# Row maxima ahead of attention, P.V in longer runs, and SyncE in written order in a fused attention and gMLP block

## The chip, the cores and the metric

The kernel runs on one core of a Trainium2 chip. The metric is device time of one execution in microseconds. TensorE (PE, with its weight loads PEld), VectorE (DVE), ScalarE (ACT), GpSimd (POOL) and SyncE (SP) run side by side; SyncE issues nearly all DMAs, ScalarE a few.

## The reference

One block over a sequence of S = 2048 rows, D = 576, in float32. `x` is normalised by row (a layer norm without weights). Side A is attention with 32 heads of 18 columns, causal with a window of 256. Side B is a gated MLP: `z = gelu(xn @ w_in)` of 4608 columns, the second half normalised by row, mixed over the sequence by `w_sp` (2048 x 2048) plus a bias, multiplied with the first half, and projected back. The result is `x + s * silu(g)`.

```python
qkv = (xn @ wqkv).reshape(B, S, 3, H, Dh)              # transposed to 3, B, H, S, Dh
scores = einsum("bhqd,bhkd->bhqk", q, k) * Dh ** -0.5  # masked to 0 <= q - k < 256
s = einsum("bhqk,bhkd->bhqd", softmax(scores), v) @ wo
z = gelu(xn @ w_in)
z1, z2 = z[..., :Fh], layernorm(z[..., Fh:])
g = (z1 * (einsum("ts,bsf->btf", w_sp, z2) + b_sp[None, :, None])) @ w_out
return x + s * silu(g)
```

## The kernel before

All large products are done in float32r with operands split in a high and a low part (ScalarE copies the high part, VectorE subtracts to get the low one), three matmuls each. The program has these stages:

1. Up to about 207 us: row norm, transposes, the q and k projection to DRAM (`st_d`) and the values to `v_d`.
2. To about 448 us: **z2**, the second half of the MLP's first projection, six column pieces (`pc`) of sixteen row blocks (`s`). Beside it GpSimd forms the four sums of `w_sp` blocks (`sp_combos`, tiles a11 to a22) that a Strassen-like spatial product needs. In the last piece, two row-maximum steps of attention unit 0 stand in each row block.
3. To about 1001 us: **attention**, in 16 units (`UNITS`: 8 groups of four heads, for the first half of the queries and then the second). A unit has 8 (first half) or 10 key blocks of four heads (`j`): 32 or 40 score items. For each, TensorE makes the transposed scores (`tps`, two PSUM buffers), ScalarE the exponential into `pt`, GpSimd the mask (two affine selects per key block), and TensorE then P.V into `ops`, four heads side by side in 32 columns each. Between the items TensorE fills in the matmuls of **z1** (`fill`, 1008 matmuls of 512 columns, in chunks of 14), the MLP's first half, whose gelu comes later.
4. To about 1697 us: the **spatial product**, 168 steps `m` of 18 matmuls (4.1 us) in three groups. Each needs a weight block `spr`, split into `sph` and `spl`, and a z block, split into `zh` and `zl`. `load_w(m + 4)` and `split_step(m + 2)` are called in step m; `pump` loads normalised z blocks (`zr`) for later products.
5. The output projections.

The **row maximum** (`row_max`) runs one unit ahead: 32 steps (4 heads, 8 query blocks), each a score matmul in `sp` (two PSUM buffers) and a masked maximum on VectorE into `mx` (`junk` takes the values); then one transpose of `mx`, its negative split in two rows (`mhl`), which go through DRAM (`m_d`) into two extra rows of the q tiles (`att<-m_d`), so that the score matmul subtracts the maximum by itself. With an empty step and the transpose a unit has `RMN = 34` steps.

The **divisor**: the values carry a column of ones, so that P.V also gives the row sums. `finish(u)` copies them out of `ou` to a tile `den` by DMA, VectorE takes the reciprocal, and that goes through DRAM (`r_d`) into a broadcast tile `rp` (of the last unit into a slot of `att`). VectorE multiplies `ou` by it, and four DMAs store to `o_d`.

The **order** in attention is written by hand for PE, POOL, DVE and ACT (`manual_schedule`): what the Python code issues first stands first on its engine. `spend` adds nominal durations to a clock, and `after(ns, fn)` issues fn once that clock has passed. SyncE is not in that list, so a scheduler places the DMAs of attention; in the spatial product SyncE stands in written order too. Each unit loads the q and k tiles of later heads with `load_pair` (eight DMAs each) into five rotating slots `att`. In a unit, the row maxima are paced over its first 70% (`RM1`), P.V blocks wait in `todo` and are issued when two are there (`PVN`), and z1 matmuls fill up to a target. Before unit 0 stand `HEAD = 28` z1 matmuls.

## Time and profile before

| | |
|---|---|
| runs | 2001.71 us median of 3 (1999.58 to 2002.24) |
| the profiled execution | 1998.85 us, span 1997.1 us, mean granted clock 0.995 |
| TensorE busy | 1954.4 us (98%) in 11096 matmuls |
| VectorE, ScalarE, GpSimd busy | 1055.0, 899.3, 289.1 us |
| spatial product, matmuls | 3 x 1008 of 128x512, idle before them 5.5 and 3.7 us |
| row maximum on VectorE | 448 of 384 columns, 553 ns each; 64 of 256 columns, 420 ns |
| exponential on ScalarE | 384 of 384 columns, 493 ns each |
| P.V matmuls | 512 of 384 columns, 448 of 256, 448 of 128 |

A row of a timeline or of the chain of waits begins with its start and its duration; the brackets give the idle time of the engine before it and what ended that. A row of waits reads: who waited for whom, microseconds in total, times, longest. PE is a matmul, PEld the weight load of the next one, which normally runs under the matmul before it. TensorE's busy time includes that its matmuls overlap, so lost time is read from the distance of one matmul's start to the next.

### The profile page before, as it was taken

To read this page: it belongs to the slowest core of one execution; us is meant where nothing else is said; L and a number is where in the kernel's file an instruction comes from. 1 tells how busy PE (TensorE), PEld (TensorE's weight loads), DVE (VectorE), ACT (ScalarE), POOL (GpSimd) and SP (SyncE) were. 2 spreads that over 40 slices of the span, in tenths; PEclk is the share of its full clock that TensorE was granted. 3 is DMA by queue.
4 is the path that set the end of the run, shared out by engine and by line. 5 is a ranking of instruction groups with operands and counts; after the bars stand their busy time and mean duration, and the time that the engine had idled before them with its cause. 6 is when DMAs were issued, how large, how long until landed. Compare 5 with 4: busy or idle time off the path is not lost.

```text
span 1997.1 us, 30611 instructions
## 1 busy us (share of the span) xinstructions
PE 1954.4 (98%) x11096; PEld 1647.0 (82%) x11096; DVE 1055.0 (53%) x2260; ACT 899.3 (45%) x1655; POOL 289.1 (14%) x360
## 2 busy tenths in 40 slices
PE   6999999999999999999999999999999999999998
PEld 5889999996777777777678887888888887999998
DVE  5411233366565656565148758676865675623222
ACT  4222322215555565656665466646554445422221
POOL 5000365102323223323200000000000000000000
PEclk9999999999999999999999999999999999999999
DMA  8655799424454655553376577857775567844441
GB/s 249 181 146 164 249 350 349 155 78 129 132 153 140 149 152 149 133 153 105 121 267 225 167 263 252 262 178 244 240 256 171 188 200 259 285 142 146 135 149 56
DMA packets 218983, 375.57 MB, mean 188 GB/s; under 512 B 43216, under 2 KB 115792, under 8 KB 218704
## 3 DMA queue, kind: packets, MB, share of 16 engines
q1 hardware_dynamic: 200880, 344.41, 55.4%
q10 hardware_dynamic: 17952, 29.21, 4.0%
q8 instruction: 87, 1.43, 0.3%
q14 instruction: 64, 0.52, 0.1%
HBM read 260.45 MB, written 112.83 MB: 187 GB/s over the span
## 4 chain that ended last, share of the span: by engine, by line
PE 85%; DMA 6%; DVE 5%; ACT 2%; issue 1%; SPq 0%; DVEq 0%; ACTq 0%
PE acc L926 27%; PE po L1018 12%; PE mm L444 11%; PE mm L650 10%; PE mm L306 5%; PE sp L394 5%; PE tps L513 5%; PE ops L536 4%; PE vps L463 3%; PE wops L988 2%; DVE spl L209 1%; DVE cb L874 1%; DVE z1t L855 1%; DMA a<-in_w_sp_dram 1%; DMA zr<-z_d 1%
## 5 line engine op out<-in xcount | busy, mean ns | idle before, releaser
L926 PE MATMUL acc<-sph,zh 128*128 128x512 f32 x1008 | 395.0, 392 | 5.5 <-ACT sph L209 5.5
L926 PE MATMUL acc<-spl,zh 128*128 128x512 f32 x1008 | 394.5, 391 | 3.7 <-DVE spl L209 3.4
L926 PE MATMUL acc<-sph,zl 128*128 128x512 f32 x1008 | 394.2, 391 | 0.0
L398 DVE CUSTOM_DVE_ANT_0 junk<-sp,band 128x384 bf16<-128x384 f32 (+1 forms) x512 | 265.5, 536 | 172.2 <-PE sp L394 164.9
L517 ACT ACTIVATE pt<-tps 128x384 f32<-128x384 f32 (+2 forms) x576 | 248.6, 439 | 179.0 <-PE tps L513 168.7
L444 PE MATMUL mm<-b,z1wh 128*128 128x512 f32 x648 | 248.4, 400 | 0.0
L926 PEld LDWEIGHTS acc<-spl,zh 128*128 128x128 f32 x1008 | 190.0, 188 | 47.5 <-DVE spl L209 7.3
L926 PEld LDWEIGHTS acc<-sph,zh 128*128 128x128 f32 x1008 | 189.9, 188 | 47.0 <-ACT sph L209 7.1
L209 DVE TENSOR_TENSOR spl<-spr,sph 128x1024 fp32r<-128x1024 f32 x166 | 202.7, 1221 | 40.0 <-ACT sph L209 39.7
L926 PEld LDWEIGHTS acc<-sph,zl 128*128 128x128 f32 x1008 | 189.8, 188 | 40.5
L513 PE MATMUL tps<-att 128*128 128x384 f32 (+1 forms) x576 | 192.5, 334 | 5.6 <-DMA att<-m_d 3.9
L650 PE MATMUL mm<-z2wh,b 128*128 128x384 f32 x720 | 192.1, 335 | 1.8 <-ACT zt L660 1.8
L394 PE MATMUL sp<-att 128*128 128x384 f32 (+1 forms) x512 | 181.8, 360 | 2.3 <-DVE mx L398 0.9
L209 ACT ACTIVATE sph<-spr 128x1024 fp32r<-128x1024 f32 x166 | 173.7, 1046 | 15.8 <-DMA spr<-in_w_sp_dram 14.9
L209 ACT ACTIVATE zh<-b 128x384 fp32r<-128x384 f32 x144 | 75.0, 521 | 197.4 <-PE acc L926 193.4
L1018 PE MATMUL po<-b,yh 128*128 128x288 f32 x896 | 155.7, 296 | 0.0
L209 DVE TENSOR_TENSOR zl<-b,zh 128x384 fp32r<-128x384 f32 x144 | 79.6, 553 | 124.8 <-ACT zh L209 124.8
L444 PE MATMUL mm<-b,z1wl 128*128 128x512 f32 x360 | 143.3, 398 | 0.0
L513 PEld LDWEIGHTS tps<-att 128*128 128x128 f32 x576 | 108.8, 189 | 41.3 <-issue 16.6
L444 PEld LDWEIGHTS mm<-b,z1wh 128*128 128x128 f32 x648 | 120.6, 189 | 25.8 <-issue 12.9
L661 DVE BATCH_NORM_STATS2 st<-zt 128x6 f32<-128x384 f32 x96 | 53.5, 559 | 166.8 <-ACT zt L660 166.8
L650 PE MATMUL mm<-z2wl,b 128*128 128x384 f32 x400 | 133.7, 334 | 0.0
(148 smaller groups left out, 2877.0 us busy)
## 6 DMA issues: line engine op xcount, KB each, us to landing
spr<-sc_d SPq DMA_DIRECT2D x96, 512.0 KB
spr<-in_w_sp_dram SPq DMA_DIRECT2D x72, 512.0 KB
zr<-z_d SPq DMA_DIRECT2D x136, 192.0 KB
st_d<-qkhl SPq DMA_DIRECT2D x72, 256.0 KB
z_d<-zt ACTq DMA_DIRECT2D x48, 384.0 KB
z1t<-z_d SPq DMA_DIRECT2D x72, 256.0 KB
y_d<-z1t SPq DMA_DIRECT2D x72, 256.0 KB
yr<-y_d SPq DMA_DIRECT2D x48, 384.0 KB
```

Source lines behind the costliest of these rows:

```text
L209: job()
L306: pe.matmul(ps, w, r, start=n == 0, stop=n == len(pl) - 1)
L394: pe.matmul(ps[:, :w], q_of(u, j)[:, i * P:(i + 1) * P], k_of(u, j)[:, k0:k0 + w], start=True, stop=True)
L398: dve.tensor_tensor_reduce(out=junk[:, :w], in0=ps[:, :w], in1=band[:, m0:m0 + w], scale=1.0, scalar=-3.0e38, op0=ALU.add, op1=ALU.max, ac ...
L444: pe.matmul(ps, w, r, start=n == 0, stop=n == len(pl) - 1)
L463: pe.matmul(ps[:, i, :288], r, w[:, i * 288:(i + 1) * 288], start=n == 0, stop=n == len(pl) - 1)
L513: pe.matmul(ps[:, :m * P], k_of(u, j)[:, (kb - base) * P:(kb - base + 1) * P], q_of(u, j)[:, (a - lo) * P:(a - lo + m) * P], start=True, s ...
L517: act.activation(pt[:, j, d0:d0 + n * P], ps[:, (qa - a) * P:(qa - a + n) * P], AF.Exp, scale=scale)
L536: pe.matmul(o_ps[c][32 * j:32 * j + 32, (lo - 4 * c) * P:(hi - 4 * c + 1) * P], vgs[u][:, kb - k0, j * VW:j * VW + 32], pt[:, j, (lo - kb) ...
L650: pe.matmul(ps[:, :ZW], r, wt, start=n == 0, stop=n == len(pl) - 1)
L926: pe.matmul(acc[j], z[:, ps], w[:, cs], start=s == i == 0 and n in OPENS, stop=s == 7 and i == 2, skip_group_check=True)
L1018: pe.matmul(po[i][:, a, :288], y[:, i * P:(i + 1) * P], w[:, a * 288:(a + 1) * 288], start=f == 0 and m == 0, stop=f == NF - 1 and m == 2)
```

## The change

**Row maximum.** All units' steps form one `stream`. It starts in the last 21 row blocks of z2 (two steps each, 42 in all: unit 0's 34 and eight, `LEAD`, of unit 1), and keeps eight steps ahead through all of attention, spread evenly over each unit. Both the fifth and the fourth slot are opened and cleared inside z2, on GpSimd, where the tiles of `sp_combos` were; so these are paced two row blocks in three instead of one in two. The maxima are stored 0.9 us of the clock behind the transpose and read back 1.8 us later. `HEAD` becomes 6.

**P.V.** `PVN` is four (two in the last unit), with five `pt` tiles. `burst` first issues the waiting `extras` and then all P.V blocks. The copy out of `ops` is issued 0.1 us of the clock later.

**extras.** The splits of the next z1 weights, the reciprocals and the divisions are put in a list, and issued at `j == 1` of each key block (one) or ahead of a run (five). The reciprocal is queued 3.6 us behind the divisor's `finish`, whose DMA stands at 0.9; before it was at 10 us. The division is queued 9.5 us behind the load of `rp`.

**SyncE** joins the written order in attention (`HEADS`), so each DMA is issued by `after` where its data should be there.

**Third spatial step.** The pool of steps 2, 5, 8... opens where the attention tiles were, `load_w(2)` and `split_step(2)` stand beside the last z1 matmuls. **pump** keeps up to four units, or five z blocks, in flight instead of two units.

```diff
-RM0 = 0.0
-RM1 = 0.70
 RMN = 34
-PVJ = 3
-PVN = 2
+LEAD = 8
+PVN = 4
+NPT = 5
-GAP = 8
-TAIL = 50 + 2 * GAP
-HEAD = 28
+GAP = 7
+TAIL = 66
+HEAD = 6
+HEADS = ENGINES | {ET.Activation, ET.SP}
...
-    def pump(n, depth=2):
+    def pump(n):
         for _ in range(n):
-            if flying and (len(flying) >= depth or not units):
-                form, got = flying.pop(0)
+            need = units[0][2] if units else 9
+            if flying and (len(flying) == 4 or sum(f[2] for f in flying) + need > 5):
+                form, got, _ = flying.pop(0)
                 form(got)
...
                 def put_max():
                     sp.dma_start(m_d[u], f32(m))
+                    after(1800, get_max)
+                def get_max():
                     rows = m_d[u].rearrange("(n j i) q -> n j (i q)", n=2, j=4)
...
-                after(500, put_max)
+                after(900, put_max)
...
+            def extra(n):
+                for _ in range(n):
+                    while extras and not extras[0]:
+                        extras.pop(0)
+                    if extras:
+                        extras[0].pop(0)()
...
                 def invert():
                     dve.reciprocal(den, den)
-                    sp.dma_start(r_d[u].rearrange("h (a b) -> (h a) b", b=HS // 32), den)
+                    after(600, lambda: sp.dma_start(r_d[u].rearrange("h (a b) -> (h a) b", b=HS // 32), den))
+                    after(2800, spread)
+                def spread():
                     sp.dma_start(rp, r_d[u].unsqueeze(1).to_broadcast([4, 32, HS]))
+                    after(9500, lambda: queue([divide]))
                 def divide():
                     dve.tensor_tensor(ou, ou, rp, ALU.mult)
+                    after(1500, store)
...
-                after(700, lambda: sp.dma_start(den, ou[DH::32, :]))
-                    after(10000, invert)
-                    after(24000, divide)
+                after(900, lambda: sp.dma_start(den, ou[DH::32, :]))
+                after(3600, lambda: queue([invert]))
...
+                stream = (step for u in range(NU) for step in row_max(u))
...
+                            if n in (4, 9) and pc * NS + s >= 6 * NS - (RMN + LEAD) // 2:
+                                next(stream)
...
+                def burst():
+                    extra(5)
+                    while todo:
+                        pv(*todo.pop(0))
+                    spend(250)
+                fill(HEAD)
...
+                        z = have + (want - have) * f - done
+                        r = min(RMN * (u + 1 + f) + LEAD, RMN * NU) - maxed
+                        while z >= 0.5 or r >= 0.5:
+                            if z >= 0.5:
                                 fill(1)
+                                z -= 1
+                            if r >= 0.5:
+                                next(stream, None)
+                                maxed += 1
+                                r -= 1
+                            if z < 1.5 and j == 3 and len(todo) >= (PVN if u < NU - 1 else 2):
+                                burst()
...
+                        if j == 1:
+                            extra(1)
...
+                work.close()
+                wpools[2] = open_pool(sets, "w2", side="right")
+                load_w(2)
+                fill(12)
+                split_step(2)
                 for _ in z1:
                     spend(MM)
...
-        for m in range(2, 4):
-            load_w(m)
+        load_w(3)
...
-            split_step(m + 2)
+            if m:
+                split_step(m + 2)
```

TensorE in the middle of a first-half unit, around a run of P.V (`ops`; `mm` is z1, `sp` the row maximum, `tps` the scores), before:

```order
L513 MATMUL tps<-att_4040 128x384
L444 MATMUL mm<-b_98,z1wh 128x512
L394 MATMUL sp<-att_1208 128x384 x2
L536 MATMUL ops<-pt,vg 32x256 x4
L536 MATMUL ops<-pt,vg 32x128 x8
L536 MATMUL ops<-pt,vg 32x256 x4
L513 MATMUL tps<-att_1210 128x384
```

and now:

```order
L526 MATMUL tps<-att_3464 128x384
L447 MATMUL mm<-b_95,z1wh 128x512
L394 MATMUL sp<-att_1205 128x384
L549 MATMUL ops<-pt_4499,vg 32x384 x4
L549 MATMUL ops<-pt_4556,vg 32x384 x4
L549 MATMUL ops<-pt,vg 32x256 x4
L549 MATMUL ops<-pt,vg 32x128 x8
L549 MATMUL ops<-pt,vg 32x256 x4
L447 MATMUL mm<-b_98,z1wh 128x512
```

A run holds the P.V of four key blocks instead of two, and the two `sp` in a row are gone: a z1 matmul stands between them.

VectorE near the end of a first-half unit, around the division (`ou<-ou,rp`; `junk` is the row maximum of one step, `mhl` the maxima of a unit, `z1wl` a weight split), before:

```order
L453 TENSOR_TENSOR z1wl<-z1raw,z1wh 128x256
L407 TENSOR_SCALAR mhl<-sp 32x128
L408 SCALAR_TENSOR_TENSOR mhl<-sp,mhl 32x128
L453 TENSOR_TENSOR z1wl<-z1raw,z1wh 128x256
L453 TENSOR_TENSOR z1wl<-z1raw,z1wh 128x128
L562 TENSOR_TENSOR ou<-ou,rp 128x1024
L398 ISA junk,mx<-sp,band 128x256
```

and now:

```order
L407 TENSOR_SCALAR mhl<-sp 32x128
L408 SCALAR_TENSOR_TENSOR mhl<-sp,mhl 32x128
L398 ISA junk,mx<-sp,band 128x256
L398 ISA mx 128x1
L398 ISA junk,mx<-sp,band 128x256
L398 ISA mx 128x1
L583 TENSOR_TENSOR ou<-ou,rp 128x1024
L398 ISA junk,mx<-sp,band 128x384
```

The division stood behind a unit's last row maximum with no other until the next unit; now it stands between two steps of the stream.

SyncE where attention ends (`spr` are weights of the spatial product, `den<-oul` the last unit's divisors, `o_d<-oul` its store), before:

```order
L567 DMA den<-oul 128x1x32
L449 DMA z_d<-z1o 128x512
L558 DMA r_d<-den 128x32
L559 DMA att_1210<-r_d 128x1x1024
L449 DMA z_d<-z1o 128x512
L565 DMA o_d<-oul 18x1024 x4
L204 DMA spr<-in_w_sp_dram 128x1024 x3
L146 DMA zr<-z_d 128x384 x2
```

and now:

```order
L205 DMA spr<-in_w_sp_dram 128x1024 x2
L589 DMA o_d<-ou 18x1024 x4
L376 DMA z_d<-z1o 128x512 x2
L205 DMA spr<-in_w_sp_dram 128x1024
L598 DMA den<-oul 128x1x32
L376 DMA z_d<-z1o 128x512
L575 DMA r_d<-den 128x32
L376 DMA z_d<-z1o 128x512
L579 DMA att_1207<-r_d 128x1x1024
L376 DMA z_d<-z1o 128x512 x2
L589 DMA o_d<-oul 18x1024 x4
L146 DMA zr<-z_d 128x384 x2
```

Three of the weight loads (steps 3, 4 and 2) stand ahead of the last divisor's transfers; the z loads still stand behind the store.

More of the change, by code (lines that the diff above doesn't have):

```diff
@@ L211 @@
     sets = ctx.enter_context(ExitStack())
-    wpools[0] = open_pool(sets, "w0", side="right")
     def split_jobs(m):
@@ L364, in load_pair @@
                     sp.dma_start(k[b + 18:b + 54, :kn], st_d[1, 0:36, h, k0:k0 + kn])
-            waiting = []
+            waiting, seen = [], []
             clock = 0.0
@@ L565, in divide, with queue @@
                         sp.dma_start(o_d[h * DH:(h + 1) * DH, cs], ou[32 * i:32 * i + DH, :])
-                after(700, lambda: sp.dma_start(den, ou[DH::32, :]))
-                if u == NU - 1:
-                    last.extend([invert, divide])
-                else:
-                    after(10000, invert)
-                    after(24000, divide)
+                def queue(jobs):
+                    if u == NU - 1:
+                        for job in jobs:
+                            job()
+                    else:
+                        extras.insert(0, jobs)
+                after(900, lambda: sp.dma_start(den, ou[DH::32, :]))
+                after(3600, lambda: queue([invert]))
             def sp_combos(stack):
@@ L600, in sp_combos @@
                         sp.dma_start(sc_d[k, q, :, cs], t)
+            spare = early.enter_context(ExitStack())
             order = early.enter_context(ExitStack())
@@ L628 @@
                 gz = open_pool(gate, "gz", bufs=2)
-                ahead = iter(())
-                combos = sp_combos(gate)
+                wcs = gate.enter_context(ExitStack())
+                combos = sp_combos(wcs)
+                stream = (step for u in range(NU) for step in row_max(u))
                 for pc in range(6):
@@ L650 @@
                             pe.matmul(ps[:, :ZW], r, wt, start=n == 0, stop=n == len(pl) - 1)
-                            if n in (4, 9):
-                                next(ahead, None)
-                        if (pc * NS + s) % 2 == 1:
+                            spend(173)
+                            if n in (4, 9) and pc * NS + s >= 6 * NS - (RMN + LEAD) // 2:
+                                next(stream)
+                        if (pc * NS + s) % 3 != 2:
                             next(combos, None)
+                        if pc * NS + s == 4 * NS + 9:
+                            for _ in combos:
+                                pass
+                            wcs.close()
+                            ab = open_pool(spare, "ab", side="right")
+                            for i in range(3, NSLOT):
+                                slots.append(ab.tile([P, SLOT], F32R, name=f"att{i}", bufs=1))
+                                pool.memset(f32(slots[i][:, 0:2 * HS]), 0.0)
+                                pool.memset(f32(slots[i][:, 2 * HS:]), 1.0)
                         if pc + 1 < 6 and s % 2 == 0:
@@ L671 @@
                             dve.bn_aggr(mv2[:, s, :], st2[:, s].rearrange("p a b -> p (a b)"))
-                for _ in ahead:
-                    pass
-                for _ in combos:
-                    pass
                 sd2 = gz.tile([P, NS], F32, name="sd2", bufs=1)
@@ L680 @@
                 dve.tensor_scalar(nmr2, nmr2, -1.0, None, ALU.mult)
-            spare = early.enter_context(ExitStack())
-            ab = open_pool(spare, "ab", side="right")
-            for i in range(3, NSLOT):
-                slots.append(ab.tile([P, SLOT], F32R, name=f"att{i}"))
-                clear(i)
             with ExitStack() as heads:
                 order.close()
-                heads.enter_context(tc.manual_schedule(engines=ENGINES | {ET.Activation}))
-                ap_ = open_pool(heads, "attn", bufs=2)
-                tps = open_pool(heads, "tps", bufs=2, space=PSUM)
-                ops = open_pool(heads, "ops", bufs=2, space=PSUM)
+                heads.enter_context(tc.manual_schedule(engines=HEADS))
+                work = heads.enter_context(ExitStack())
+                ap_ = open_pool(work, "attn", bufs=2)
+                tps = open_pool(work, "tps", bufs=2, space=PSUM)
+                ops = open_pool(work, "ops", bufs=2, space=PSUM)
                 load_v(0)
@@ L699 @@
                     tick()
-                    if u == 0:
-                        fill(HEAD)
                     if u == NU - 1:
+                        while todo:
+                            fill(GAP)
+                            pv(*todo.pop(0))
                         spare.close()
-                        pre = open_pool(sets, "pre", side="right")
-                        wpools[1] = pre
+                        wpools[0] = open_pool(sets, "w0", side="right")
+                        wpools[1] = pre = open_pool(sets, "pre", side="right")
                         homes[0] = (pre, "z0")
@@ L750 @@
                         tick()
-                    for _ in ahead:
-                        fill(1)
                 while prep:
@@ L757 @@
                     pv(*todo.pop(0))
-                clock += 100000
-                tick()
-                fill(4)
-                for job in last:
-                    job()
+                while extras:
+                    extra(1)
+                fill(1)
+                work.close()
[3 more added lines that the diff above has]
+                split_step(2)
                 for _ in z1:
                     spend(MM)
+                while waiting:
+                    spend(2000)
     ow = open_pool(ctx, "ow")
@@ L806, in load @@
                 return raw
-            return load, lambda raw: split(h, l, raw)
+            return load, lambda raw: split(h, l, raw), 1
         def o_unit():
-            return lambda: wo_load(ow, 0), lambda raw: ohls.setdefault(0, wo_split(ow, raw))
+            return lambda: wo_load(ow, 0), lambda raw: ohls.setdefault(0, wo_split(ow, raw)), 1
         def free_tile(n):
```

60 lines of the change are left out of this document (24 added, 36 removed).

## The prediction

> **What bounds the kernel now.** I read four views in this order: the chain of waits on the page, then the granted clock by windows, then the waits of the attention stage (448 to 980 us), then single stretches of the timeline.
>
> ```profile
> PE 85%; DMA 6%; DVE 5%; ACT 2%; issue 1%; SPq 0%; DVEq 0%; ACTq 0%
> ```
>
> TensorE sets the time. The change adds and removes no matmul, so all it can move is lost issue time: idle time, and matmuls that start later than the one before allows. The waits show where:
>
> ```profile
> PE acc L926 <- ACT sph L209: 5.5, 3, 4.5
> PE tps L513 <- DMA att<-m_d: 3.9, 1, 3.9
> PEld sp L394 <- DVE mx L398: 36.6, 138, 0.9
> PEld tps L513 <- ACT pt L517: 13.8, 39, 0.8
> 458.00:464.00 6.00, 5.63 (x17) 4.54 (x17) 3.00 (x13) 2.52 (x6) 0.79 (x2) 0.56 0.70 179
> 1009.00:1017.00 8.00, 6.82 (x17) 5.11 (x18) 4.61 (x5) 6.13 (x9) 0.00 (x0) 0.57 0.81 284
> ```
>
> (In the window rows the third figure from the end is the granted clock.) Two idles of about 4 us, at both ends of attention, are each followed by a stretch at about half clock: it loses (1 - 0.56) x 6 = 2.6 us after the first and (1 - 0.57) x 8 = 3.4 us after the second. Between them no idle is long, but two patterns repeat. The first is a weight load that waits for VectorE's row maximum:
>
> ```profile
> 853.87 0.34 PE L513 MATMUL tps<-att 128*128 128x384 f32 x1
> 854.04 0.39 PE L444 MATMUL mm<-b,z1wl 128*128 128x512 f32 x1
> 854.39 0.45 PE L394 MATMUL sp<-att 128*128 128x384 f32 x1
> 854.68 0.39 PE L444 MATMUL mm<-b,z1wh 128*128 128x512 f32 x1
> 854.91 0.34 PE L513 MATMUL tps<-att 128*128 128x384 f32 x1
> 854.39 0.19 PEld L394 LDWEIGHTS sp<-att 128*128 128x128 f32 x1 [0.33 <-DVE mx L398]
> ```
>
> Undisturbed, a 384-wide matmul takes 0.17 us to the next start (853.87 to 854.04) and a 512-wide one 0.23 (854.68 to 854.91). Here the 512-wide one takes 0.35, and the late 384-wide one, whose weight load nothing covers, 0.29: 0.12 + 0.12 = 0.24 us lost for 0.33 us of idle weight load. The 138 waits have a mean of 36.6 / 138 = 0.265, so each costs about 0.17, together **23 us**. The second pattern is a run of P.V:
>
> ```profile
> 499.87 0.34 PE L394 MATMUL sp<-att 128*128 128x384 f32 x1
> 500.14 1.50 PE L536 MATMUL ops<-pt,vg 128*32 128x384 f32 x16
> 501.56 0.44 PE L513 MATMUL tps<-att 128*128 128x384 f32 x1
> 500.49 0.13 PEld L536 LDWEIGHTS ops<-pt,vg 128*32 128x32 f32 x4 [0.19 <-issue]
> 500.81 0.13 PEld L536 LDWEIGHTS ops<-pt,vg 128*32 128x32 f32 x4 [0.19 <-issue]
> ```
>
> A group of four takes 0.32 us (500.49 to 500.81), four groups 1.28; the run takes 1.42 (500.14 to 501.56). Going in costs 0.27 - 0.17 = 0.10, the run itself 0.14, and the first matmul behind it has an uncovered weight load, 0.12 as above: about 0.35 us a run, however long.
>
> **The change part by part**, against the profiled execution (1998.85 us; span 1997.1; the median of the runs shown, 2001.71, is 2.9 above it).
>
> *Runs of four.* The order has 73 runs of P.V before and 41 now: 32 x 0.35 = **-11**.
>
> *Start of attention.* Row maxima of unit 0 now end four row blocks before the second projection does, so the 3.9 us wait and the 2.6 us behind it go. What is late next is ScalarE, which loses the cover of 22 of 28 z1 matmuls:
>
> ```profile
> 447.94 0.49 ACT L660 ACTIVATE zt<-mm 128x384 f32<-128x384 f32 x1 [2.28 <-PE mm L650]
> 448.86 1.28 ACT L116 ACT_TABLE_LOAD   x1 [0.43 <-ACT zt L660]
> 447.75 0.39 PE L444 MATMUL mm<-b,z1wh 128*128 128x512 f32 x1
> ```
>
> This load ends at 450.1 and a small square root follows. With the second table load directly behind it, at about 450.5, the first exponential ends near 450.5 + 1.3 + 0.5 = 452.3. TensorE leaves the projection at 447.75, runs six z1 matmuls (1.4), and reaches the third score, which needs that exponential's PSUM buffer, about 450.4: a new stall of 1.9. Sum -3.9 - 2.6 + 1.9 = **-4.6**. The Trainium skill (ScalarE: Activation LUTs, "What ACT_TABLE_LOAD costs") adds a drain of 1.38 us to each switch; the trace disagrees, since only 0.43 us lies before the load. By the page this part would come to about -2 instead.
>
> *Row maximum.* It costs 23 us now because 34 steps stand in 70% of a unit. Spread evenly, a step has about 0.8 us of TensorE time against 0.55 + 0.08 on VectorE. Summing intervals along the order, a step needs about 1.2 us from the start of the step two before it (two PSUM buffers); 267 of 495 steps had less, 42 of 487 have less now: 42 x 0.17 = 7. So -16 from this. But the last 30% of a unit had no row maxima, and VectorE's other work stood there; now it stands between row maxima:
>
> ```profile
> L398 DVE CUSTOM_DVE_ANT_0 junk<-sp,band 128x384 bf16<-128x384 f32 x448 | 240.2, 553 | 137.9 <-PE sp L394 132.2
> L562 DVE TENSOR_TENSOR ou<-ou,rp 128x1024 f32<-128x1024 f32 x15 | 20.4, 1363 | 10.9 <-DMA rp<-r_d 10.8
> 889.99 5.76 DMA den<-ou
> 895.85 0.35 DVE L557 RECIPROCAL den<-den 128x32 f32<-128x32 f32 x1 [1.18 <-DMA den<-ou]
> 895.73 0.40 PE L444 MATMUL mm<-b,z1wh 128*128 128x512 f32 x1
> 896.67 0.45 PE L394 MATMUL sp<-att 128*128 128x384 f32 x1 [0.55 <-DVE mx L398]
> ```
>
> The division (1.36) delays the next row maximum by about as much, less 0.1 to 0.5 of slack: 1.3 in the seven units of the first half, 0.9 in four of the second, nothing in the others, where a P.V run covers it: **+12**.
>
> The reciprocal is worse. It stood at least 9.3 us behind its transfer by the kernel's clock; now it is 2.7 us plus the wait for the next slot, about 4. The row above is the price of one that comes too early: VectorE waits 1.18, and TensorE takes 0.94 (895.73 to 896.67) instead of 0.23, then 0.12 for the uncovered load, so 0.83 for 1.18: the wait less 0.35. How long the transfer takes is bounded by two rows, 5.76 above with traffic, and under 2.4 at the end, where the next transfer follows it:
>
> ```profile
> 775.17 0.29 SPq L361 DMA_DIRECT2D att<-st_d  x1
> 782.97 0.29 SPq L364 DMA_DIRECT2D att<-st_d  x1
> 785.01 0.57 SPq L567 DMA_DIRECT2D den<-ou  x1
> 986.23 0.56 SPq L567 DMA_DIRECT2D den<-oul  x1
> 988.65 0.39 SPq L558 DMA_DIRECT2D r_d<-den  x1
> ```
>
> I take 5, near the loaded row, because SyncE in program order issues it right behind the sixteen loads of the next two pairs (7.8 us of issue, 775.17 to 782.97). It then leaves about 8 us after the unit's start and lands at 13. VectorE reaches the reciprocal at about 11.4 in the first half and at 10.0 in every other unit of the second (the kernel's clock puts it 10.0 and 8.75 behind the unit's start; the rest is lag): waits of 1.6 and 3.3, prices (1.6 - 0.35) x 7 + (3.3 - 0.35) x 3 = 17.6: **+18**. Landing after 2.4 it is 1; after 7 it is 38. Row maximum in all: -16 + 12 + 18 = **+14**.
>
> *Scores waiting for ScalarE.* Evictions issued behind the next work, and stalls in which ScalarE catches up: 13.8 us of idle weight load in 39 waits, of which I take a third off at the price above: **-3** (bounds 0 and -8).
>
> *SyncE's order at unit starts.* The row of maxima is written back 2.9 us behind the transposes by the kernel's clock and needed 2.5 us later; with o_d stores ahead of it in some units I add **+1** (0 to +15).
>
> *Third spatial step.* Before, its weights waited for the last division:
>
> ```profile
> 991.92 8.81 DMA att<-r_d
> 1000.83 1.24 DVE oul L562
> 1003.55 5.04 DMA spr<-in_w_sp_dram
> 1008.61 1.06 ACT sph L209
> 1009.70 1.24 DVE spl L209
> ```
>
> Now they load beside z1. That removes 4.5 + 0.5 of wait and 3.4 of half clock. Late next: steps 3 to 5, whose VectorE split stands behind the division and whose loads or first z blocks stand behind the o_d stores. By these durations the division ends about 21 us behind the last P.V, step 3's split 1.8 later, and TensorE needs it at 24; I allow 1: **-7.4** (bounds -8.4 and 0).
>
> *Deeper prefetch of z blocks.* The stretch around 1200 us loses 3 us now:
>
> ```profile
> 1195.00:1250.00 55.00, 52.05 (x223) 41.20 (x222) 45.03 (x70) 35.05 (x53) 0.00 (x0) 1.00 0.72 242
> ```
>
> With up to four units in flight most of it goes: **-2.5** (0 to -3). The rest (w_sp sums and memsets moved within the second projection) lies beside TensorE's matmuls, which lose next to nothing there, and I cost it at 0; uncovered, the two memsets of an attention slot (3328 columns) would cost about 4.4 at the division's rate of 1.36 for 1024, an estimate.
>
> Sum: -11 - 4.6 + 14 - 3 + 1 - 7.4 - 2.5 = **-13.5**. The profiled execution would take 1985.3, the median of runs **1988**.
>
> **The rivals.**
>
> *The divisors land in time.* If den takes 2.4 us although loads stand ahead of it, 17 of the 18 falls away: 1988 - 17 = 1971; with the divisions covered too, 1959. For it: 16 KB is little. Against it: 5.76 us at 889.99.
>
> *VectorE's waits decide, to the other side.* Same place, the reciprocal: each further us of landing costs ten units a us. From 1.4 us more than I take, the gain is gone; at 2.5 more the time is 1988 + 25 = 2013. For it: the queue is fullest at a unit's start. Against it: the loaded row is 5.76, not 7.5.
>
> *Half clock behind those waits.* An idle of 2.56 us early in the program was already followed by one:
>
> ```profile
> 36.37 0.88 PE L289 MATMUL tpt<-ident,xr 128*128 128x128 f32 x3 [2.56 <-DVE xr L283]
> 36.50:40.00 3.50, 3.50 (x15) 3.06 (x15) 2.06 (x5) 0.91 (x2) 3.46 (x5) 0.51 0.15 32
> ```
>
> It lost 0.49 x 3.5 = 1.7. Three such stalls in the second half up to all ten would add 5 to 17: about 1998, no change. The Trainium skill (TensorE: Matmul & The Clock Gate, "The HAM clock gate") asks for an idle window of about 3.4 us; the trace has it after less.
>
> *SyncE's program order holds the row of maxima.* A us lost at each of fifteen unit starts: 1988 + 14 = 2002, no change. Against it: this wait shows once now.
>
> **How the numbers follow.** Forecast 0.45 (1976 to 1997); divisors in time 0.23; reciprocals to the other side 0.17; half clock 0.09; maxima held 0.06. A measurement here tells about 0.2%, 4 us, from no change, so faster means under 1997.7. Faster: most of the forecast, all of the second, half of the half-clock case: 0.70. Same 0.12, slower 0.18. The range reaches half into the cases on both sides: 1957 to 2008.
>
> **What would show it.** P.V: as many runs as the order has, and 0.35 us at each. Start: no wait for att<-m_d, one of about 2 us for pt. Row maximum: far fewer than 138 weight-load waits, but some over 1 us, each next to a RECIPROCAL with idle time before it from den, or to an ou division. If the longest waits of sp stay under 0.5, the +18 is wrong and the time is near 1971. Joint: no 4.5 us wait at the third step and full clock. Waits of tps for att<-m_d at unit starts would make the last rival right.

## The result and the profile after

The changed kernel takes 2064.28 us (median of 4 runs, 2060.88 to 2067.82) against 2001.97 before: a ratio of 1.0312, 95% interval 1.0289 to 1.0336. It is **62 us slower**; 1988 was forecast, with a range up to 2008. Its profiled execution took 2066.54 us, span 2064.8.

The chain of waits of the changed kernel (shares of the span):

```profile
PE 73%; DMA 14%; DVE 7%; ACT 3%; issue 2%; SPq 1%; ACTq 0%; POOL 0%; DVEq 0%; POOLq 0%
```

TensorE's share fell from 85 to 73%, that of transfers rose from 6 to 14. Its waits (who waited for whom, microseconds, times, longest):

```profile
PE sp L394 <- DVE mx L398: 26.5, 14, 4.4
PE acc L964 <- ACT sph L210: 22.0, 6, 5.6
PE tps L526 <- ACT pt L530: 21.7, 13, 6.1
PE sp L394 <- DMA att<-st_d: 6.9, 7, 2.4
PE acc L964 <- DVE spl L210: 5.8, 10, 0.8
PE tps L526 <- DMA att<-m_d: 1.5, 3, 0.5
```

Before, the sum of such waits in attention and the spatial product was about 15 us; it is 84 now. The mean granted clock fell from 0.995 to 0.979: 1.6% of 2065 is up to 33 us more, about half of the loss: time at half clock, most of it behind those idles.

By stage, counted in both profiled executions from the last matmul of one stage to the last of the next: the second projection ends 7.9 us later (at 455.5 us, before 447.6), attention with z1 is 40.4 longer (589.5, before 549.1), the spatial product 26.1 longer (729.7, before 703.6), and the rest 6.7 shorter (see the last section).

Behind VectorE and ScalarE stands SyncE. One unit's start, first its queue, then VectorE (start, duration, and in brackets the idle time before and what ended it):

```profile
493.24 0.34 SPq L361 DMA_DIRECT2D att<-st_d  x1
...
495.86 0.33 SPq L364 DMA_DIRECT2D att<-st_d  x1
497.01 0.29 SPq L361 DMA_DIRECT2D att<-st_d  x1
...
501.50 0.29 SPq L364 DMA_DIRECT2D att<-st_d  x1
502.66 0.65 SPq L598 DMA_DIRECT2D den<-ou  x1
503.35 0.47 SPq L425 DMA_DIRECT2D z1raw<-in_w_z_dram  x1
```

```profile
507.62 0.35 DVE L574 RECIPROCAL den<-den 128x32 f32<-128x32 f32 x1 [3.68 <-DMA den<-ou]
```

SyncE issues the first eight of sixteen loads in 2.9 us and the other eight in 4.8: the ninth goes out only at 497.01, when the first has landed. `den` and the z1 weights (`z1raw`) stand behind them. At two other units `z1raw` stands ahead of `den`, and ScalarE stops at the split:

```profile
676.28 0.36 SPq L425 DMA_DIRECT2D z1raw<-in_w_z_dram  x1
```

```profile
682.50 0.42 ACT L483 ACTIVATE z1wh<-z1raw 128x256 fp32r<-128x256 f32 x1 [7.13 <-DMA z1raw<-in_w_z_dram]
```

In the spatial product SyncE stands too, at `zr` loads, and what is behind them comes late; its queue, then ScalarE, then TensorE:

```profile
1071.78 10.97 SPq L146 DMA_DIRECT2D zr<-z_d  x4
...
1085.47 1.84 SPq L881 DMA_DIRECT2D z1t<-z_d  x4
```

```profile
1090.57 1.32 ACT L889 ACTIVATE z1t<-z1t 128x512 f32<-128x512 f32 x2 [5.49 <-DMA z1t<-z_d]
```

```profile
1093.30 0.80 PE L964 MATMUL acc<-sph,zh 128*128 128x512 f32 x1 [3.03 <-ACT sph L210]
```

Four loads that need some 0.45 us each to issue take 10.97. ScalarE's wait for `z1t` holds up the split of the next weights, queued behind it.

### The profile page after: what moved, and what is told of

Same layout as the page of the kernel before. It is cut to its first block, busy times and chain, and to the rows that moved or that the text cites. A ratio compares the mean times of both kernels' runs of the same rounds, so it can differ in the third digit from the quotient of the medians.

```text
span 2064.8 us, 30616 instructions
## 1 busy us (share of the span) xinstructions
PE 1948.8 (94%) x11096; PEld 1672.1 (81%) x11096; DVE 1058.7 (51%) x2258; ACT 897.4 (43%) x1655; POOL 285.6 (14%) x362
## 4 chain that ended last, share of the span: by engine, by line
PE 73%; DMA 14%; DVE 7%; ACT 3%; issue 2%; SPq 1%; ACTq 0%; POOL 0%; DVEq 0%; POOLq 0%
PE acc L964 24%; PE po L1057 11%; PE mm L678 10%; PE mm L447 8%; PE mm L306 5%; PE tps L526 3%; PE ops L549 3%; PE sp L394 3%; DMA att<-st_d 3%; PE vps L465 2%; DMA z1t<-z_d 2%; DMA den<-ou 2%; DMA z1raw<-in_w_z_dram 1%; DVE spl L210 1%; PE wops L1027 1%
## 5 line engine op out<-in xcount | busy, mean ns | idle before, releaser
L398 DVE CUSTOM_DVE_ANT_0 junk<-sp,band 128x384 bf16<-128x384 f32 (+1 forms) x512 | 272.1, 538 | 181.9 <-PE sp L394 178.2
L447 PE MATMUL mm<-b,z1wh 128*128 128x512 f32 x648 | 258.7, 409 | 0.0
L526 PE MATMUL tps<-att 128*128 128x384 f32 (+1 forms) x576 | 193.7, 336 | 23.6 <-ACT pt L530 21.7
L394 PE MATMUL sp<-att 128*128 128x384 f32 (+1 forms) x512 | 177.1, 346 | 33.6 <-DVE mx L398 26.5
L526 PEld LDWEIGHTS tps<-att 128*128 128x128 f32 x576 | 112.6, 195 | 48.1 <-ACT pt L530 35.7
L447 PEld LDWEIGHTS mm<-b,z1wh 128*128 128x128 f32 x648 | 126.1, 195 | 27.9 <-issue 7.2
L533 POOL TENSOR_SCALAR_AFFINE_SELECT pt<-pt 128x512 f32<-128x512 f32 x128 | 83.1, 649 | 462.4 <-ACT pt L530 462.4
```

The costliest lines, as they stand in the source:

```text
L394: pe.matmul(ps[:, :w], q_of(u, j)[:, i * P:(i + 1) * P], k_of(u, j)[:, k0:k0 + w], start=True, stop=True)
L398: dve.tensor_tensor_reduce(out=junk[:, :w], in0=ps[:, :w], in1=band[:, m0:m0 + w], scale=1.0, scalar=-3.0e38, op0=ALU.add, op1=ALU.max, ac ...
L447: pe.matmul(ps, w, r, start=n == 0, stop=n == len(pl) - 1)
L526: pe.matmul(ps[:, :m * P], k_of(u, j)[:, (kb - base) * P:(kb - base + 1) * P], q_of(u, j)[:, (a - lo) * P:(a - lo + m) * P], start=True, s ...
L533: pool.affine_select(out=pt[:, :, 0:P], in_=pt[:, :, 0:P], pattern=[[0, 4], [1, P]], compare_op=ALU.is_ge, fill=0.0, base=0, channel_multi ...
```

## The experiments

In every group the kernel before took 2001.2 to 2002.3 us. I began with one cause per part: the deeper pump makes SyncE wait for buffers (Theory A of pump_two), and the splits and reciprocals stand too close behind their transfers, each by itself. The rival is that the row of transfers decides, and a stall taken away comes back at the next consumer.

**1. One part undone at a time.** `pump_two` forms a unit as soon as two are in flight, as before:

```diff
-            if flying and (len(flying) == 4 or sum(f[2] for f in flying) + need > 5):
+            if flying and (len(flying) >= 2 or not units):
```

> The changed kernel with one part undone: pump keeps two units in flight again. Theory A: the stalls of the spatial product come from the deeper pump. With up to five z blocks in flight and six buffers, SyncE, which stands in written order, waits for a buffer (52.6 us for L146 against 13.8 before), the z1t and spr loads behind it go out late, ScalarE waits for z1t (62.7 us against 25.3) and TensorE for sph and spl (27.8 us) with half clock behind it (about 27 us at half speed, 13.6 lost). Undone, these 41 us go and the 5 us that the stretch at 1200 us lost before come back: 2064 - 36 = 2028 (2020 to 2036). Rival: the z1t loads are late for another reason (they are asked for at the same place in both kernels, and the stage starts with other loads in the queue), and the time moves by less than 8 us.

Measured 2029.92 (2027.08 to 2031.63): **-34**. Theory A holds; SyncE's wait at L146 is 10.3 us in place of 52.6, and the spatial product takes 693.0 us in place of 729.7. `split_late` puts the splits of the next z1 weights back where they stood:

```diff
-                            if c == 1 and n == 7 and f + 1 < FH // P:
-                                extras.append(nxt[2])
+                            if f + 1 < FH // P and c in (2, 3) and n in (1, 5, 9):
+                                nxt[2].pop(0)()
```

> The changed kernel with one part undone: the splits of the next z1 weights stand at fixed z1 matmuls of the third and fourth chunk again, 10 to 20 matmuls later, not in the list of extras. Theory A: the three longest idles of TensorE (5.6 at 469, 5.4 at 640, 6.4 at 677 us) are ScalarE's, which stands at z1wh until z1raw lands (20.7 us in 5 waits); they go with the 20 us of half clock behind them, less the reciprocals that are then late at the same two places (about 3 us each): 2064 - 20 = 2044 (2037 to 2052). Rival: the transfers that stand behind sixteen pair loads decide by themselves, and ScalarE or VectorE waits as long at the next place: less than 8 us.

Measured 2058.59 (2048.89 to 2062.10): -6, the rival's figure, and hardly clear of the scatter. `rec_late` queues the reciprocal later:

```diff
-                after(3600, lambda: queue([invert]))
+                after(8000 if u < NU - 1 else 3600, lambda: queue([invert]))
```

> The changed kernel with one part moved: the reciprocal of every unit but the last is queued 8 us of the clock behind finish instead of 3.6. Theory A: VectorE's wait for den (32 us in 8 waits beside the last unit's 18) is the cause of most of the 26.5 us in which TensorE waits for mx, and of seven half clock stretches of 3.4 to 6.8 us (27 us, 13.6 lost): 2064 - 32 = 2032 (2025 to 2042). Rival: half of these stalls stand at divisions or at other VectorE work that also waits for SyncE, and the time falls by less than 12 us.

Measured 2065.72 (2064.78 to 2068.26): **no gain**, though the waits for `mx` that it was to take away are gone. TensorE's and ScalarE's waits in attention in this kernel:

```profile
PE tps L526 <- ACT pt L530: 36.1, 16, 5.5
PE sp L394 <- DMA att<-st_d: 15.0, 7, 2.6
PE sp L394 <- DVE mx L398: 1.2, 4, 0.4
```

```profile
ACT z1wh L483 <- DMA z1raw<-in_w_z_dram: 41.5, 9, 6.6
```

26.5 us became 1.2, but the wait for `pt` grew from 21.7 to 36.1 and that for the pair loads from 6.9 to 15.0. A TensorE that no longer stops for `den` meets `z1raw` earlier. So the stalls of attention are not independent; Theory B of the next group took that up. `sync_free` takes SyncE out of the written order:

```diff
-HEADS = ENGINES | {ET.Activation, ET.SP}
+HEADS = ENGINES | {ET.Activation}
```

> The changed kernel with one part undone: SyncE is not in the written order of attention, a scheduler places its DMAs as before. Theory A: the two sorts of stalls in attention have one cause, the sixteen loads of two pairs (8 us of issue) that stand ahead of z1raw and den in the written order; a scheduler that issues den and z1raw between them takes most of both away: 2064 - 40 = 2024 (2010 to 2040). Rival: the distances in the order of VectorE and ScalarE are too short for any transfer at that load, and the time moves by less than 10 us, or gets longer where the scheduler puts a row of maxima late.

Measured 2053.36 (2047.63 to 2059.59): -11, beside both. The waits for `z1raw` are gone, those for `den` stay.

**2. Both waits at once, and the row of loads.** `both_late` is pump_two, split_late and rec_late together.

> Pump back to two units, z1 splits back at their fixed places, and the reciprocal at 8 us of the clock: what pump_two, split_late and rec_late did one by one. Theory B (after those three: a wait that is taken away alone comes back at the next instruction whose transfer stands behind the sixteen pair loads): den and z1raw now both have the time, so TensorE's waits for mx and pt (42 us in pump_two, with 15 to 20 us of half clock) go nearly all, and only its waits for the pair loads themselves stay (8 us there): 2030 - 40 = 1990 (1983 to 2002). Rival: the wait moves on once more, to the pair loads (15 us in rec_late, more here) or the row of maxima, because SyncE's row is late as a whole: over 2010.

Measured 2002.56 (1994.32 to 2010.48, 10 runs), ratio 1.0004 (0.9989 to 1.0019). The two that gave -6 and +1 alone give **-27** together. That isn't owed to the pump: both_late_four_blocks, in the third group, has both of them and still the pump's stalls, and is 23 us under the changed kernel. What stays is SyncE's (ScalarE stands 15.7 us in 8 waits for `z1raw`, and TensorE for its `pt`):

```profile
PE sp L394 <- DMA att<-st_d: 17.0, 8, 3.3
PE tps L526 <- ACT pt L530: 14.2, 14, 2.5
PE tps L526 <- DMA att<-m_d: 4.9, 3, 2.7
```

`pairs_apart` is pump_two with the second pair load later:

```diff
-                    for p in (2 * u + 3, 2 * u + 4):
-                        if p < 2 * NU:
-                            load_pair(p)
+                    if 2 * u + 3 < 2 * NU:
+                        load_pair(2 * u + 3)
...
+                        if t == 14 and 2 * u + 4 < 2 * NU:
+                            load_pair(2 * u + 4)
```

> Pump back to two units, and only this beside it: of the two pair loads at a unit's start the second is issued at the fifteenth score item, so that eight loads stand ahead of den and z1raw instead of sixteen. Splits and reciprocals stay where the change put them. Theory B: the block of sixteen is the root; den and z1raw leave SyncE about 5 us earlier, and most of 42 us of waits with their half clock go: 2030 - 30 = 2000 (1992 to 2010). Rival: the reciprocal stands 2.7 us of the clock behind its transfer and the transfer takes 3.7 us and more even then, so VectorE still waits 1 to 2 us in each unit: 2015 to 2025.

Measured 2030.09 (2025.79 to 2032.84): nothing against pump_two. VectorE's waits for `den` did go, all but the last unit's, so the sixteen loads were their cause. But the eight loads now meet another transfer. SyncE's queue, and TensorE:

```profile
601.58 0.54 SPq L579 DMA_DIRECT2D rp<-r_d  x1
602.17 0.49 SPq L361 DMA_DIRECT2D att<-st_d  x1
...
606.71 0.27 SPq L363 DMA_DIRECT2D att<-st_d  x1
613.83 0.29 SPq L364 DMA_DIRECT2D att<-st_d  x1
```

```profile
617.98 0.58 PE L394 MATMUL sp<-att 128*128 128x256 f32 x1 [4.41 <-DMA att<-st_d]
```

The broadcast `rp<-r_d` (512 KB) takes 12.2 us to land, and the eighth load behind it goes out only then.

`both_late_pairs` is both_late and pairs_apart.

> both_late and pairs_apart together. Theory B: every transfer has its time, except the first pair load of a unit, which the stream of maxima needs eight steps earlier than before: 1985 (1978 to 1993), under the kernel before. If the terms of the prediction that the other stalls hid (P.V in longer runs -9 to -11, third step -7, start -4, row maxima -16) are real, this kernel shows them: TensorE's waits for mx, pt and att together under 12 us in attention. Rival: the eight steps of lead put the pair load on the path by themselves, and the time stays at 1995 or above.

Measured 2012.98 (2005.08 to 2019.70): 10 more than both_late. With the later load in the queue the row of maxima is late, 15.0 us in 10 waits for att<-m_d against 4.9 in 3.

`both_late_runs_of_two` sets `PVN = 2`.

> both_late_pairs with P.V in runs of two blocks instead of four. By the price of 0.26 to 0.35 us a run that the kernel before and the changed one show, 30 runs more cost 8 to 11 us over both_late_pairs. Rival: shorter runs leave VectorE and ScalarE less to catch up behind, each stall of a run is cover for a division or a mask, and the difference is under 3 us.

Measured 2015.98 (2012.38 to 2019.85), 3 over both_late_pairs, which is the rival's figure and within the scatter of both.

**3. SyncE without its row; the parts alone.** `both_late_sync_free` is both_late and sync_free.

> both_late with SyncE out of the written order, so that a scheduler places the DMAs of attention. Theory C (what is left in both_late is SyncE's row: TensorE waits 17 us for att<-st_d, 5 for att<-m_d and 14 for pt while ScalarE stands at z1wh for z1raw): the late issues go, as the waits for att<-st_d and z1raw did in sync_free; 2002 - 20 = 1982 (1975 to 1992). Rival: the transfers themselves are the limit (one queue, emptied in order), so the waits change their names only: within 6 us of 2002.

Measured **1978.30** (1969.86 to 1980.90), ratio 0.9877 (0.9857 to 0.9898). Theory C holds: SyncE's written order alone costs 24 us, once the other causes are gone, and the rest of the change is worth 24 us against the kernel before. Its waits:

```profile
PE sp L394 <- DMA att<-st_d: 13.6, 6, 5.7
PE tps L526 <- ACT pt L530: 4.7, 8, 1.8
PE tps L526 <- DMA att<-m_d: 4.1, 7, 1.2
```

```profile
PEld sp L394 <- DVE mx L398: 10.0, 15, 1.8
```

`both_late_four_blocks` is both_late with the changed pump and a lower limit:

```diff
-            if flying and (len(flying) == 4 or sum(f[2] for f in flying) + need > 5):
+            if flying and (len(flying) == 4 or sum(f[2] for f in flying) + need > 4):
```

> both_late, but with the changed pump, held to four z blocks in flight instead of five (still up to four units). Theory A in its narrow form (SyncE waits because five of six buffers are in flight): with two buffers free, as in the kernel before, the stalls of the spatial product do not come, and the stretch at 1200 us may gain its 2 us: 2001 (1996 to 2006). Rival: the number of units ahead is the cause (the z loads take the queue ahead of z1t and spr): 2015 to 2036.

Measured 2041.09 (2038.10 to 2043.00), the rival's range; SyncE waits as in the changed kernel:

```profile
SPq L146 <- DVE zr L158: 52.1, 12, 9.1
```

The narrow form of Theory A isn't tested by this, because the edit doesn't hold four blocks. Working the function through, call by call, shows why: it forms at most one unit for each that it loads. When the units come to have two blocks (`k == 1`), the blocks in flight go to 5, 6, 7, 8 whatever the limit, out of six buffers. A load's buffer is then freed by a form that stands a step behind it. `held_five`, in the next group, tests that.

`before_third` gives the kernel before the third step's new place, and nothing else:

```diff
+                fill(4)
+                work.close()
+                wpools[2] = open_pool(sets, "w2", side="right")
+                load_w(2)
+                fill(12)
+                split_step(2)
                 clock += 100000
                 tick()
-                fill(4)
```

> The kernel before with one part of the change: the pool of the third spatial step opens where the attention tiles were, and its load and split stand beside the last z1 matmuls. By the prediction's term the joint gains 7.4 us (0 to 8.4): 2001.5 - 7.4 = 1994 (1992 to 1997). Rival: without SyncE in written order the load goes out no earlier, or steps 3 to 5 are late in its place: under 3 us.

Measured 1988.76 (1984.22 to 1993.58), ratio 0.9940 (0.9923 to 0.9958): -13, more than expected. 40 us behind the joint, of the kernel before and of this one:

```profile
1003.00:1043.00 40.00, 35.07 (x141) 28.06 (x141) 17.42 (x23) 25.25 (x38) 0.00 (x0) 0.91 0.81 281
```

```profile
995.00:1035.00 40.00, 40.00 (x177) 32.91 (x176) 15.22 (x19) 22.41 (x36) 0.00 (x0) 1.00 0.72 245
```

36 matmuls more at 0.227 us are 8.2 us. The rest is not explained by the joint: in the profiled executions attention is as long as before (549.1 us), the spatial product 7.9 us shorter, and the output projection 5.8 (see the last section).

`before_third_runs` adds P.V in runs of four, with five `pt` tiles.

> before_third with P.V in runs of four blocks and five pt tiles beside it; the row maxima, the divisors, the splits and SyncE stay as they were. By the prediction's term 32 runs fewer gain 11 us, by the two profiles' own price of 0.23 to 0.26 us a run 8: 1994 - 9 = 1985 (1982 to 1988). Rival: with row maxima in the first 70% of a unit the longer runs collide with VectorE's row or with the masks, and under 4 us are left.

Measured 1991.64 (1983.55 to 1998.12): no gain over before_third. In the profiled executions (here it was the slowest run) attention takes 554.0 us, against 549.1 there. It is the rival's result, by another wait; before_third has one of 4.1 us here:

```profile
PE tps L516 <- DMA att<-m_d: 12.1, 9, 4.1
```

**4. Mechanisms one by one, on both_late_sync_free.** `held_five`:

```diff
-            if flying and (len(flying) >= 2 or not units):
+            while flying and (len(flying) == 4 or sum(f[2] for f in flying) + need > 5):
                 form, got, _ = flying.pop(0)
                 form(got)
+                if not units:
+                    break
```

> both_late_sync_free with the changed pump, but so that the limit of five blocks holds: it forms as many units as needed before each load (while in place of if). As written it forms one unit for each load, and eight blocks come to be asked for out of six buffers, in both_late_four_blocks as well; the buffer of a load is then freed by a form that stands a step behind it, and SyncE, in order, stands there. Theory A, in this form: with the limit held no such load exists, the stalls of the spatial product (35 us) do not come, and the 5 us stretch at 1200 us may shrink by 0 to 4: 1978 - 2 = 1976 (1971 to 1981). Rival: the later forms as such are the cause (ScalarE and VectorE reach them too late for the steps): 1995 to 2015.

Measured 1985.92 (1982.18 to 1991.13). Most of the 35 us does not come, so the limit that was not held is the main cause; but 8 us more than with two units is outside what was expected. They lie in the last group, 1540 to 1700 us, where SyncE and ScalarE now wait. Up to there the spatial product is 1.7 us ahead of both_late_sync_free's. The new waits:

```profile
SPq L846 <- DVE b L113: 35.6, 6, 11.2
SPq L816 <- DVE ohl L826: 18.5, 2, 12.8
```

```profile
ACT sph L212 <- DMA spr<-sc_d: 11.1, 3, 5.3
```

L846 loads output weights into a ring of two tiles, L816 into one tile, while four such units may be in flight: the same fault in other rings. (In both_late_sync_free, with two units in flight, the two are 24.3 and 2.2, and ScalarE has no such wait.)

`free_runs_of_two` has `PVN = 2`:

> both_late_sync_free with P.V in runs of two blocks. By the price of a run in the traces (0.23 to 0.26 us) some 30 runs more cost 8 us: 1986 (1983 to 1990). Rival: as between both_late_pairs and both_late_runs_of_two (3 us), and as in before_third_runs (where waits for att<-m_d, 12.1 us against 4.1, took the gain), shorter runs cost under 4 us, because each run is followed by a wait of another kind that a shorter one makes shorter.

Measured 1977.75 (1971.23 to 1980.49): **no difference**. The waits of TensorE with runs of two:

```profile
PE sp L394 <- DMA att<-st_d: 8.4, 6, 1.8
PE tps L526 <- ACT pt L530: 3.6, 7, 1.8
PE sp L394 <- DVE mx L398: 1.9, 5, 0.7
```

Against the rows of both_late_sync_free, `att<-st_d` is 5.2 less and the 4.1 for `att<-m_d` are gone: 9.3 us, about what the 33 runs more (74 against 41) cost at 0.3 each.

`free_reciprocal_early` has the reciprocal at 3.6 us again:

> both_late_sync_free with the reciprocal back at 3.6 us of the clock. With SyncE out of the written order and the splits late, this is the price of the early reciprocal alone. In sync_free VectorE waited 40 us for den in 12 waits beside the last unit's, and TensorE 34 us for mx in 17: theory: +25 to +45 with the half clock behind these waits, 1978 + 35 = 2013. By the prediction's own term (18 us, at 0.35 less than each wait, without half clock): 1996. Rival: without the sixteen loads ahead den lands in time, under 8 us.

Measured 2012.00 (2008.97 to 2015.76): **+34**, as the theory had it. The last unit's wait for `den` (13.4) is in the first row, as it is in both_late_sync_free (14.4).

```profile
DVE den L574 <- DMA den<-ou: 52.3, 14, 13.4
```

```profile
PE sp L394 <- DVE mx L398: 33.2, 18, 5.2
```

`free_split_early` has the early splits again:

> both_late_sync_free with the splits of z1's weights back in the list of extras. In sync_free the wait of ScalarE for z1raw was gone and TensorE's for pt was 4.5 us. Theory C: with SyncE free the early split costs nothing: 1978 (1973 to 1984). Rival: z1raw is asked for one chunk before its split whatever SyncE does, and ScalarE waits for it in some units: 1986 to 1996.

Measured 1977.83 (1974.17 to 1986.63): nothing. So the early split costs time only with SyncE in written order, where `z1raw` is late.

`free_lead_six` and `free_lead_four` have `LEAD = 6` and `LEAD = 4`:

> both_late_sync_free with the stream of row maxima six steps ahead instead of eight. Theory D: the lead is squeezed between two transfers. With eight the stream reaches the heads of the pair that is loaded at the unit's start too early (TensorE waits 13.6 us for att<-st_d in 6), with fewer the row of maxima (the last read of m_d goes out 3.7 to 7.7 us behind the transpose) is late for the next unit's first score: two steps are about 1.7 us, so the first falls by 5 to 8 us and the second (4.1 us) grows by 10 to 15: 1978 + 5 = 1983 (1976 to 1990). Rival: the maxima have room to spare, and the time falls to 1970 or below.

Measured **1971.74** (1967.80 to 1974.70), ratio 0.9843 (0.9819 to 0.9868): the best version here, 30 us under the kernel before. (Against both_late_sync_free it is 7 us in the medians, with runs that overlap; in the profiled executions attention is 11.0 us shorter, 527.8 against 538.8.) Theory D's mechanism is there, its balance was off: the waits for `att<-st_d` (13.6) are all gone, and those for the maxima grow by 8, not 10 to 15.

```profile
PE tps L526 <- DMA att<-m_d: 11.8, 10, 1.8
```

> The same with four steps. Theory D: the waits for att<-st_d are nearly gone, but each of fifteen units waits 1 to 3 us for att<-m_d, 25 to 40 us with the half clock behind some of them: 1978 + 20 = 1998 (1985 to 2015). Rival: under 1978.

Measured 2012.64 (2008.97 to 2017.33). In the second unit of this kernel the read-back of the maxima stands behind the first score (479.40 us), so that one waits for none and is computed with other maxima: this kernel leaves out a dependence, and isn't one to use. The unit's second score waits 10.8 us, and the first scores of the thirteen units behind it 28.6 together:

```profile
PE tps L526 <- DMA att<-m_d: 39.4, 14, 10.8
```

## Why the prediction was wrong

By the runs, the loss adds up in the order in which I undid the parts: pump 34, early splits and reciprocals 27, SyncE's order 24, and two steps of lead 7: 2064 - 92 = 1972. In another order the shares differ: undone alone, the splits are worth 6, the reciprocals nothing and SyncE's order 11. The prediction's terms, one by one:

- **Deeper pump, -2.5 (0 to -3): the step that failed most**, +34. It took the limit of five blocks as the code states it and asked what more prefetch gains. It did not count buffers against loads in the order in which SyncE reaches them, nor ask what stands behind a load that waits, though the six buffers and the one form for each load stand in the code. The gain that it priced is there where the limit is held: 1.7 us in held_five, up to the last group.
- **SyncE's order, +1 (0 to +15):** 24, behind the others, and the wrong victim. The maxima, which the last rival named, were in time (1.5 us in 3 waits); `z1raw` and the pair loads were late. The reciprocal's part named `den` behind sixteen loads, but no part named the weights of z1, which go through the same row, and whose splits the change had moved forward. That move has no term at all.
- **Reciprocals, +18:** the place, the cause and the sign were right, 34 measured alone. The landing was sized well: by 502.66 and 507.62, 5.0 us. The waits were sized too short: SyncE issued this `den` 9.4 us behind the unit's first load, not 8, and VectorE was there at 503.94 (507.62 - 3.68), 10.7 behind it, not 11.4, so that it waited 3.7 and not 1.6. The term had ten waits, 21.1 us together; free_reciprocal_early has 13 beside the last unit's, 38.9 us. At the prediction's price (each wait less 0.35) that is 34, and TensorE's waits for `mx` grew by 31.6 (33.2 against 1.6), while its waits for transfers and `pt` fell by 12.8. Half clock comes on top: 30.0 us of it against 14.9, some 7.5 lost. It stood as a rival with 5 to 17 us and should have been part of the term. The rival that put this case at 2013 is near free_reciprocal_early (2012) by chance: it had a longer landing as its reason.
- **Evening out the row maximum, -16:** held, by its waits. 36.6 us of late weight loads in 138 waits became 10.0 in 15 (both_late_sync_free). But the eight steps of lead, which had no term, brought the waits for the pair loads; two steps less are worth 7. **Divisions, +12** (by its own figures 1.3 x 7 + 0.9 x 4 = 12.7): mis-sized. What was to be left of the even stream and the divisions was 7 + 12 = 19; in both_late_sync_free these 15 waits bound both at 10 us of idle weight load, less than 9 at the prediction's price (0.24 lost for 0.33).
- **Runs of four, -11:** the runs are as many as the order has, but three comparisons of four with two give 3 us less, 3 us more and no difference, none clear of the scatter. That the waits for transfers grew by as much is measured in two of them (9.3 us, and 8.0 for `att<-m_d` in before_third_runs); that a faster TensorE meets transfers whose pace SyncE sets is the likely reading, not shown by a run of its own.
- **Start of attention, -4.6:** the 3.9 us wait is gone, and one of 1.8 us for `pt` stands there in both_late_sync_free, as the prediction had it (1.9). In the changed kernel one of 1.7 stands there, and behind it one of 5.2, for a `z1raw` that was issued at 467.46.
- **Scores waiting for ScalarE, -3:** no gain: idle weight load 13.8 us in 39 waits before, 35.7 in 36 in the changed kernel, 18.1 in 35 in both_late_sync_free, about 2 of it the wait at the start.
- **Third step, -7.4:** held, 8.2 by the matmul counts.
- **Moves within the first stages, 0:** the second projection ended 7.9 us later in the changed kernel, which the prediction had at nothing. TensorE's waits between 150 and 330 us are 2.6 and 3.6 there against 1.8 before, and two stretches of 3.4 us at half clock (at 194.6 and 283.3) lose 3.4, which together is most of it. The cost isn't steady: in rec_late, whose code is the same up to there, the stage ended at 450.8, 3.2 later than before. No run took these moves apart.

The common error: each part was priced against the engines' queues of the kernel before, and the queue in which the change made the order fixed, SyncE's, was priced for two transfers only, `den` and the row of maxima. Gains and stalls were added as if independent; the runs show that a stall taken away alone can give nothing.

## What to carry to other kernels

When a DMA-issuing engine is put in written order, list for every transfer what stands ahead of it, and how many may be in flight; each consumer then needs that whole delay, and consumers that share the queue must be moved together, since freeing one alone can hand the wait to the next. A prefetch depth is a count of buffers at the moment of each load: if the code frees one unit for each it takes, units of unequal size break the limit. Price every idle of TensorE near 2 us or more with the half clock that can follow it.

## What the hardware showed

**The clock goes by slots.** Half clock comes in stretches of 3.4, 6.8 or 10.2 us that begin on a grid of 3.41 us. Slots of the changed kernel, each followed by the next one (second figure: TensorE's busy time; third from the end: the clock):

```profile
539.35:542.77 3.42, 1.62 (x9) 1.10 (x7) 1.01 (x6) 1.16 (x3) 1.22 (x2) 1.00 0.74 184
542.77:546.18 3.41, 3.41 (x18) 3.03 (x19) 2.56 (x11) 2.57 (x6) 0.38 (x1) 1.00 0.70 187
573.49:576.90 3.41, 1.56 (x8) 1.09 (x7) 1.79 (x7) 1.03 (x4) 1.22 (x2) 1.00 0.43 138
576.90:580.31 3.41, 3.41 (x12) 3.04 (x11) 1.59 (x8) 1.64 (x4) 0.61 (x2) 0.50 0.73 164
```

In attention, full-clock slots with 1.58 us of busy time or more kept the clock, those with 1.56 or less halved the next: 1.7 us lost each time. The Trainium skill (TensorE: Matmul & The Clock Gate, "The HAM clock gate") has the free-running window of about 3.4 us, and the trace agrees; it asks for an idle window, and here a slot that was 46% busy was enough. So it matters whether an idle of 2 us falls into one slot or across two.

**Two speeds of the output projection.** Its 1728 matmuls run at 133.3 ns apiece in eighteen of the twenty profiled executions and at 130.0 in two, at a granted clock of 1.00 in both. A hundred microseconds of before and of before_third:

```profile
1800.00:1900.00 100.00, 100.00 (x752) 100.00 (x751) 4.94 (x14) 1.00 0.45 143
```

```profile
1800.00:1900.00 100.00, 100.00 (x771) 100.00 (x770) 4.92 (x14) 1.00 0.51 158
```

That is 5.8 us for one program stage that no part touches, in the profiled executions of the changed kernel and of before_third alone. It may be part of before_third's 13; how often the timed runs have it isn't known, and no cause was found. Differences of under 6 us between the runs above can't be told from it.
